# Computing k transposed, with its row sums on VectorE and a DMA transpose back to rows

## The chip, the cores and the metric

The kernel runs on one core of a Trainium2 chip. The metric is the device time of one execution in microseconds (us), of the slowest core (here there is only one). The profile's span is about 2 us shorter than that time.

## The reference, cut to what matters

A transformer block with adaptive layer norm: linear attention, then a gated feed-forward. Sequence 2048, width 1024, 32 heads of 32, bf16. The change concerns the attention's k:

```python
phi = lambda t: jnp.where(t > 0, t + 1, jnp.exp(t)) + 1e-06
pq, pk = (phi(q), phi(k))
kv  = jnp.einsum('bhsd,bhse->bhde', pk, v)
z   = jnp.einsum('bhsd->bhd', pk)                 # sum of phi(k) over all tokens
num = jnp.einsum('bhqd,bhde->bhqe', pq, kv)
den = jnp.einsum('bhqd,bhd->bhq', pq, z)[..., None] + 1e-06
o   = num / den
```

## The kernel before

A helper records every operation of every engine in program order, works out the semaphore waits from the tiles that they touch, and then emits each engine's list. So every engine, and the one DMA queue that SP feeds, works strictly in the recorded order. All profile lines carry the helper's line number (L178); tiles tell them apart.

The q/k stage works in four chunks of 512 tokens. For each chunk it needs `HT` (called h below): the normalised input (`XRES`, 128 tokens by 1024), transposed by four DMA transposes of 256 KB, then scaled and shifted tile by tile (8 tiles, 128x512), by VectorE and ScalarE. `HT` has two buffers, so h of chunk n+1 is prepared while chunk n is multiplied. A group is 8 matmuls of 128x512; a chunk is 8 groups for k, then 8 for q. Each group's PSUM bank is evacuated by ScalarE twice (exp and relu) and VectorE joins the two, for two groups at a time:

```python
def phi_flush():
    for i, dst in phi_pend:       # E1 = min(exp, 1) + 1e-6
        P.dve("tensor_scalar", out=E1[:, i, :], in0=E1[:, i, :], scalar1=1.0, scalar2=1e-6,
              op0=ALU.min, op1=ALU.add)
    for i, dst in phi_pend:       # phi = relu + E1
        P.dve("tensor_tensor", out=dst, in0=RL[:, i, :], in1=E1[:, i, :], op=ALU.add)
    ...
def k_group(ch, j, h):            # k by rows: tokens on partitions
    ...
    for dt in range(NDT):
        P.pe("matmul", out=PS[:, bank, :], lhsT=HT[:, buf, dt, j * 128:(j + 1) * 128],
             rhs=WQK[:, dt, lo:lo + 512], start=(dt == 0), stop=(dt == NDT - 1))
    phi_evac(bank, PKH[h][:, st, :])

def z_mm(st):                     # z: one-column matmuls against ones, 8 for each 128 tokens
    for hg in range(NHG):
        P.pe("matmul", out=PS[:, 6, 32 + hg:33 + hg], lhsT=PKH[hg // 4][:, st, (hg % 4) * 128:(hg % 4 + 1) * 128],
             rhs=ONES[:, 0:1], start=mcol_first[0], stop=(st == NST - 1), skip_group_check=True)
...
def late_loads():                 # called once, during chunk 0: 6 MB
    for ch in range(2, NCH):
        P.dma("x%d" % ch, XRES[:, 4 * ch:4 * ch + 4, :], xv[:, 4 * ch:4 * ch + 4, :])
    P.dma("stg0", STG[:], wmv[:, :, 2048:3072])
    P.dma("wv", WV[:], wqkvv[:, :, 2048:3072])
```

Between the groups stand side jobs, by group number. Those of chunk 1 that matter here: normalise the tokens of chunk 2 and send them to the DMA transpose (`ln1_xn`, `th_dma`, after groups 6 and 7), and scale the 8 tiles of h (`th_mod`, after groups 10 to 14). In chunk 2 the same for chunk 3, from group 1 on.

After the q/k stage come the products of k with the input (`pk`, called the attention products here), the denominator, the output projection and the feed-forward.

## Time and profile before

| | before |
|---|---|
| time, median | 840.5 us |
| TensorE busy | 829.9 of 837.9 us |
| VectorE busy | 299.7 us |
| one-column matmuls for z | 128, in 16 groups of 8 |

The engine table of the page (busy time, share of the span, instructions):

```profile
PE 829.9 (99%) x4241; PEld 383.6 (46%) x4241; DVE 299.7 (36%) x641; ACT 203.8 (24%) x355; POOL 40.9 (5%) x52
```

TensorE is the bound: 99% busy, and the chain of waits was 96% TensorE. The stage windows (columns: stretch, length, then busy time of PE, PEld, DVE, ACT and POOL with their instruction counts, granted clock, DMA share, GB/s) show that VectorE (DVE) is nevertheless close to full in parts of the q/k stage. The one before chunk 3:

```profile
89.70:103.90 14.20, 14.20 (x82) 6.64 (x81) 13.85 (x28) 11.12 (x20) 0.00 (x0) 1.00 0.12 31
```

The timeline of TensorE before (start, length, what; runs of like instructions merged, names are output, moving and stationary operand): the start of the last full-width q products of chunk 0, the start of chunk 2, one group for z, and the first attention product. The stretch between the first and the last of these lines, 26.26 to 132.94 = 106.68 us, is the yardstick. (Some expected texts below measure from the k products on, which start 28 matmuls later: 100.53 us before.)

```profile
26.26 6.31 PE L178 MATMUL ps<-ht,wqk 128*128 128x512 bf16 x28
...
75.45 8.80 PE L178 MATMUL ps<-wqk,ht 128*128 128x512 bf16 x40
...
91.39 0.24 PE L178 MATMUL ps<-ones,pk_87 128*128 128x1 bf16 x4
91.50 0.24 PE L178 MATMUL ps<-ones,pk_88 128*128 128x1 bf16 x4
91.60 3.61 PE L178 MATMUL ps<-ht,wqk 128*128 128x512 bf16 x16
...
132.94 2.32 PE L178 MATMUL ps<-pk_87,xres 128*128 128x512 bf16 x10
```

A group for z delays what follows from 91.39 to 91.60. The lengths printed for the matmuls are modelled and overlap; starts are what to count with.

How h of chunk 2 came in. The queue of SP first (the same kind of answer for the DMA issues; the length is that of the issuing), then VectorE's first scaling of that h:

```profile
59.97 2.61 SPq L178 DMA_TRANSPOSE ht<-xres  x2
```
```profile
63.58 3.66 SPq L178 DMA_TRANSPOSE ht<-xres  x2
```
```profile
69.17 0.41 DVE L178 TENSOR_SCALAR ht<-ht,modcol 128x512 bf16<-128x512 bf16 x1 [1.75 <-DMA ht<-xres]
```

The brackets say how long the engine was idle before that instruction, and for what. There was a gap in the queue between the two pairs of transposes, and VectorE waited 1.75 us for the last one to land. No TensorE wait followed from it: chunk 2 starts at 75.45 with 40 matmuls without a break.

### The profile page before, as it was taken

What the parts mean: (1) busy time and instruction counts of PE and PEld (TensorE: products, weight loads), DVE (VectorE), ACT (ScalarE), POOL (GpSimd) and SP (SyncE); (2) the same over time, 40 slices, a digit from 0 to 9 for tenths busy, and PEclk for the clock granted to TensorE, in tenths of its full rate; (3) what the DMA queues carried; (4) which work ended last, traced back from release to release, by engine and by line L of the source; (5) the groups of instructions that cost most, each with busy time, mean ns of one, the idle gap of its engine ahead of it and who ended that gap; (6) DMA issues with size and microseconds to landing.
All of it is one profiled execution on the core that took longest, in us unless ns stands there. A gap on an engine that the chain in (4) does not pass through costs nothing.

```text
span 837.9 us, 10302 instructions
## 1 busy us (share of the span) xinstructions
PE 829.9 (99%) x4241; PEld 383.6 (46%) x4241; DVE 299.7 (36%) x641; ACT 203.8 (24%) x355; POOL 40.9 (5%) x52
## 2 busy tenths in 40 slices
PE   7999999999999999999999999999999999999998
PEld 4444444454444444444444444444444444444444
DVE  5777966566984222111221112022121202111111
ACT  4667753223333111110111111021111111111111
POOL 1000000000050000030000003000000300000000
PEclk9999999999999999999999999999999999999999
DMA  9992323757096895530355562045557104553000
GB/s 283 265 322 48 75 77 127 162 147 273 29 251 187 254 308 154 154 73 26 111 153 151 151 162 58 20 114 151 151 151 181 45 13 114 151 152 98 1 25 26
DMA packets 178125, 112.99 MB, mean 135 GB/s; under 512 B 32664, under 2 KB 161824, under 8 KB 178080
## 3 DMA queue, kind: packets, MB, share of 16 engines
q1 hardware_dynamic: 178080, 112.35, 48.3%
q8 instruction: 33, 0.54, 0.3%
q14 instruction: 12, 0.10, 0.0%
HBM read 100.67 MB, written 4.33 MB: 125 GB/s over the span
## 4 chain that ended last, share of the span: by engine, by line
PE 96%; SPq 2%; DMA 1%; DVE 1%; issue 0%; ACT 0%; DVEq 0%
PE ps L178 96%; SPq L178 2%; DMA wsa<-in_w_mod_dram 1%; DVE acc L178 0%; DVE xres L178 0%; DVE mhl L178 0%; ACT mw L178 0%; DVE ve_72 L178 0%; DVE ut L178 0%; DVE mean_70 L178 0%; DVE msq_71 L178 0%; DVE sumx L178 0%; DVEq L249 0%
## 5 line engine op out<-in xcount | busy, mean ns | idle before, releaser
L178 DVE TENSOR_TENSOR at<-sg,ps 128x512 bf16<-128x512 bf16 x112 | 77.0, 687 | 296.2 <-PE ps L178 296.2
L178 ACT ACTIVATE sg<-ps 128x512 bf16<-128x512 f32 x112 | 66.9, 597 | 310.3 <-PE ps L178 310.3
L178 PE MATMUL ps<-wd_a,at 128*128 128x512 bf16 (+2 forms) x528 | 113.5, 373 | 0.0
L178 PE MATMUL ps<-wd_b,at 128*128 128x512 bf16 (+2 forms) x396 | 85.8, 373 | 0.0
L178 PEld LDWEIGHTS ps<-wd_a,at 128*128 128x128 bf16 x528 | 51.1, 98 | 59.8
L178 DVE TENSOR_TENSOR ut<-att,gb_b 128x512 bf16<-128x512 bf16 (+1 forms) x32 | 14.4, 451 | 166.7 <-ACT att L178 166.7
L178 ACT ACTIVATE att<-ps 128x512 bf16<-128x512 f32 (+1 forms) x32 | 17.4, 591 | 182.1 <-PE ps L178 182.1
L178 PE MATMUL ps<-ht,wqk 128*128 128x512 bf16 (+1 forms) x266 | 58.2, 371 | 0.6 <-DVE ht L178 0.6
L178 PEld LDWEIGHTS ps<-wd_b,at 128*128 128x128 bf16 x396 | 38.3, 98 | 44.7
L178 PE MATMUL ps<-wqk,ht 128*128 128x512 bf16 x256 | 57.4, 379 | 0.0
L178 PE MATMUL ps<-mw,pqt 128*128 128x512 bf16 x256 | 56.2, 379 | 0.1
L178 PE MATMUL ps<-h2t,gug_114 128*128 128x512 bf16 x224 | 52.9, 379 | 0.0
L178 PE MATMUL ps<-h2t,gug_111 128*128 128x512 bf16 x224 | 52.9, 379 | 0.0
L178 PE MATMUL ps<-h2t,guu_117 128*128 128x512 bf16 x224 | 52.9, 379 | 0.0
L178 PE MATMUL ps<-h2t,guu_116 128*128 128x512 bf16 x224 | 52.9, 379 | 0.0
L178 PE MATMUL ps<-h2t,guu_118 128*128 128x512 bf16 x224 | 52.9, 379 | 0.0
L178 PE MATMUL ps<-h2t,guu_115 128*128 128x512 bf16 x224 | 52.9, 379 | 0.0
L178 PE MATMUL ps<-h2t,gug_112 128*128 128x512 bf16 x224 | 52.9, 379 | 0.0
L178 PE MATMUL ps<-h2t,gug_113 128*128 128x512 bf16 x224 | 52.9, 379 | 0.0
L178 POOL TENSOR_SCALAR h2t<-h2t,modcol 128x512 bf16<-128x512 bf16 x32 | 28.2, 896 | 394.3 <-DMA h2t<-xn_119 394.3
L178 ACT ACTIVATE e_92<-ps 128x512 bf16<-128x512 f32 x64 | 39.1, 610 | 30.8 <-PE ps L178 26.9
L178 ACT ACTIVATE rl<-ps 128x512 bf16<-128x512 f32 x64 | 38.9, 608 | 0.0
(120 smaller groups left out, 686.9 us busy)
## 6 DMA issues: line engine op xcount, KB each, us to landing
gug_111<-in_B_w_gate_dram SPq DMA_DIRECT2D x14, 512.0 KB, 4.1
guu_115<-in_B_w_up_dram SPq DMA_DIRECT2D x14, 512.0 KB, 5.3
gug_112<-in_B_w_gate_dram SPq DMA_DIRECT2D x14, 512.0 KB, 4.0
guu_116<-in_B_w_up_dram SPq DMA_DIRECT2D x14, 512.0 KB, 5.3
gug_113<-in_B_w_gate_dram SPq DMA_DIRECT2D x14, 512.0 KB, 4.3
guu_117<-in_B_w_up_dram SPq DMA_DIRECT2D x14, 512.0 KB, 5.5
gug_114<-in_B_w_gate_dram SPq DMA_DIRECT2D x14, 512.0 KB, 4.1
guu_118<-in_B_w_up_dram SPq DMA_DIRECT2D x14, 512.0 KB, 5.3
```

The source lines that it names most:

```text
L178: return getattr(e, method)(**kw)
```

## The change

The intent: take the 16 groups of z matmuls off the bounding engine. If k is computed transposed, as q is, then the sum over tokens runs along the free dimension, and VectorE can produce it as a by-product of the last addition. But the attention products need k by rows, so each half chunk (4 groups, 512 KB) goes back through one DMA transpose. The loads of 6 MB are cut into pieces and spread, so that the transposes can pass between them.

```diff
+        PKT = [T("pkt%d" % i, o_, [128, 4, 4, 128], BF16) for i, o_ in enumerate((200 * KB, SM + 3072))]
+        ZP = T("zp", SM + 7808, [128, NHG, 4], FP32)
...
             for i, dst in phi_pend:
-                P.dve("tensor_tensor", out=dst, in0=RL[:, i, :], in1=E1[:, i, :], op=ALU.add)
+                if isinstance(dst, tuple):
+                    ch, nt = dst
+                    pkt = PKT[nt // 4]
+                    rows = lambda t_: t_[:, i, :].rearrange("p (j q) -> p j q", j=4)
+                    P.dve("scalar_tensor_tensor", out=pkt[:, :, nt % 4, :], in0=rows(RL), scalar=1.0, in1=rows(E1),
+                          op0=ALU.mult, op1=ALU.add, accum_out=ZP[:, nt, ch:ch + 1])
+                    if nt % 4 == 3:
+                        xbar(PKH[nt // 4][:, 4 * ch:4 * ch + 4, :].rearrange("p j (n d) -> p (j n) d", d=128),
+                             pkt[:].rearrange("p j n q -> p (j n q)"))
+                else:
+                    P.dve("tensor_tensor", out=dst, in0=RL[:, i, :], in1=E1[:, i, :], op=ALU.add)
...
-        def k_group(ch, j, h):
+        def k_group(ch, nt):
...
-                P.pe("matmul", out=PS[:, bank, :], lhsT=HT[:, buf, dt, j * 128:(j + 1) * 128],
-                     rhs=WQK[:, dt, lo:lo + 512], start=(dt == 0), stop=(dt == NDT - 1))
-            phi_evac(bank, PKH[h][:, st, :])
+                P.pe("matmul", out=PS[:, bank, :], lhsT=WQK[:, dt, D + nt * 128:D + (nt + 1) * 128],
+                     rhs=HT[:, buf, dt, :], start=(dt == 0), stop=(dt == NDT - 1))
+            phi_evac(bank, (ch, nt))
...  (z_mm and its calls go; z_cols reduces ZP over the chunks, late in chunk 3)
-        add(kside, 1, late_loads)
+        for i in range(4):
+            add(kside, i, lambda i=i: x_load(8 + i))          # 256 KB each
...
+        for i in range(4):
+            add(s1, 2 * i, lambda i=i: x_load(12 + i))
+        for i in range(NDT):
+            add(s1, 8 + i, lambda i=i: stg_load(i))
+            add(s2, 1 + i, lambda i=i: wv_load(i))
...  (two small modulation steps move to later places)
```

`s1`, `s2`, `s3` are the side jobs of chunks 1 to 3. The k transpose is recorded right after the last addition of its half chunk, so its place in the SP queue is fixed there. For chunk 1 that is between the second and the third of the h transposes for chunk 2.

More of the change, by code (lines that the diff above doesn't have):

```diff
@@ L330, in bass_adaLN_cond__linear_attn_block__swiglu_ffn__prompt_kernel @@
         MASK4 = T("mask4", SM + 2368, [128, 4], BF16)
-        BQ = T("bq", SM + 7808, [128, NDT], FP32)
         SUMXH = T("sumxh", SM + 2816, [128, NST, 2], FP32)
@@ L417, in bass_adaLN_cond__linear_attn_block__swiglu_ffn__prompt_kernel, with x_load, stg_load, wv_load @@
         P.dma("wk1", WQK[:, :, 1536:2048], wqkvv[:, :, 1536:2048])
-        def late_loads():
-            for ch in range(2, NCH):
-                P.dma("x%d" % ch, XRES[:, 4 * ch:4 * ch + 4, :], xv[:, 4 * ch:4 * ch + 4, :])
-            P.dma("stg0", STG[:], wmv[:, :, 2048:3072])
-            P.dma("wv", WV[:], wqkvv[:, :, 2048:3072])
+        def x_load(st):
+            P.dma("x%d" % st, XRES[:, st, :], xv[:, st, :])
+        def stg_load(kt):
+            P.dma("stg0_%d" % kt, STG[:, kt, :], wmv[:, kt, 2048:3072])
+        def wv_load(kt):
+            P.dma("wv%d" % kt, WV[:, kt, :], wqkvv[:, kt, 2048:3072])
         P.pool("memset", ap=IDENT[:], constant=1.0)
@@ L682, in q_group @@
             phi_evac(bank, PQT[:, nt, ch * 512:(ch + 1) * 512])
-        def k_group(ch, j, h):
-            st = 4 * ch + j
+        def k_group(ch, nt):
             buf, bank = ch % 2, next_bank()
-            lo = D + h * 512
             for dt in range(NDT):
-                P.pe("matmul", out=PS[:, bank, :], lhsT=HT[:, buf, dt, j * 128:(j + 1) * 128],
-                     rhs=WQK[:, dt, lo:lo + 512], start=(dt == 0), stop=(dt == NDT - 1))
-            phi_evac(bank, PKH[h][:, st, :])
-        mcol_first = [True]
+                P.pe("matmul", out=PS[:, bank, :], lhsT=WQK[:, dt, D + nt * 128:D + (nt + 1) * 128],
+                     rhs=HT[:, buf, dt, :], start=(dt == 0), stop=(dt == NDT - 1))
+            phi_evac(bank, (ch, nt))
         def macc(src, kt):
@@ L711, in mod_cols @@
                          rhs=ONES[:, 0:1], start=(m == 0 and i == 0), stop=(i == 1), skip_group_check=True)
-        def z_mm(st):
-            for hg in range(NHG):
-                P.pe("matmul", out=PS[:, 6, 32 + hg:33 + hg], lhsT=PKH[hg // 4][:, st, (hg % 4) * 128:(hg % 4 + 1) * 128],
-                     rhs=ONES[:, 0:1], start=mcol_first[0], stop=(st == NST - 1), skip_group_check=True)
-                mcol_first[0] = False
         def mod_fin_col(bank, c0, idx, plus_one):
@@ L807, in bass_adaLN_cond__linear_attn_block__swiglu_ffn__prompt_kernel @@
         q_phase_chunk0(qside)
-        gi = 0
-        for h in range(2):
-            for j in range(4):
-                k_group(0, j, h)
-                for f in kside.get(gi, []):
-                    f()
-                gi += 1
+        for gi in range(8):
+            k_group(0, gi)
+            for f in kside.get(gi, []):
+                f()
         def chunk(ch, side):
@@ L818, in chunk @@
                 if gi < 8:
-                    k_group(ch, gi // 2, gi % 2)
+                    k_group(ch, gi)
                 else:
@@ L823, in chunk, with z_cols @@
                     f()
-        s1, s2, s3 = {}, {}, {}
-        for j in range(4):
-            add(s1, 1 + j, lambda j=j: z_mm(j))
-            for ch, s_ in ((1, s1), (2, s2), (3, s3)):
-                add(s_, 4 + 2 * j, lambda st=4 * ch + j: z_mm(st))
+        def z_cols():
+            P.dve("tensor_reduce", out=ZCOL[:], in_=ZP[:], axis=mybir.AxisListType.X, op=ALU.add)
+            P.dve("tensor_copy", out=ZHL[:, 0, :], in_=ZCOL[:])
+            P.dve("tensor_tensor", out=ZHL[:, 1, :], in0=ZCOL[:], in1=ZHL[:, 0, :], op=ALU.subtract)
+            P.dve("tensor_tensor", out=ZSEL[:].rearrange("p (g x) -> p g x", x=36)[:, :, 0:4],
+                  in0=ZHL[:, 0, :].unsqueeze(2).to_broadcast([128, NHG, 4]),
+                  in1=MASK4[:].unsqueeze(1).to_broadcast([128, NHG, 4]), op=ALU.mult)
+        s1, s2, s3 = {}, {}, {}
+        for i in range(4):
[3 more added lines that the diff above has]
+            add(s2, 1 + i, lambda i=i: wv_load(i))
         ops = []
@@ L860, in bass_adaLN_cond__linear_attn_block__swiglu_ffn__prompt_kernel @@
         add(s3, 3, lambda: mod_row_a(7, 0, 0))
-        add(s3, 6, lambda: mod_row_b(7, 0, GA_B))
+        add(s3, 12, lambda: mod_row_b(7, 0, GA_B))
+        add(s3, 10, z_cols)
         chunk(1, s1)
@@ L865, in bass_adaLN_cond__linear_attn_block__swiglu_ffn__prompt_kernel @@
         phi_flush()
-        P.dve("tensor_copy", out=ZCOL[:], in_=PS[:, 6, 32:40])
         P.dma("wo", WO[:], wov)
-        P.dve("tensor_copy", out=ZHL[:, 0, :], in_=ZCOL[:])
-        P.dve("tensor_tensor", out=ZHL[:, 1, :], in0=ZCOL[:], in1=ZHL[:, 0, :], op=ALU.subtract)
-        P.dve("tensor_tensor", out=ZSEL[:].rearrange("p (g x) -> p g x", x=36)[:, :, 0:4],
-              in0=ZHL[:, 0, :].unsqueeze(2).to_broadcast([128, NHG, 4]),
-              in1=MASK4[:].unsqueeze(1).to_broadcast([128, NHG, 4]), op=ALU.mult)
         G_BANKS = [0] + [next_bank() for _ in range(4)]
@@ L977, in bass_adaLN_cond__linear_attn_block__swiglu_ffn__prompt_kernel @@
                 z_row()
+            if g == 1:
+                den()
+            if g == 3:
                 mod_cols(7, 0)
                 mod_fin_col(7, 0, 2, True)
-            if g == 1:
-                den()
             if 6 <= g <= 9:
```

## The prediction

> **What bounds it now.** TensorE. The engine table gives PE 829.9 us of an 837.9 us span (99%), at full granted clock; the chain of waits is 96% PE. VectorE (299.7 us, 36%) is off the chain on average, but windows of the q/k stage show it close: busy 17.4 of 18.8 us (28.4-47.2), 13.9 of 14.2 (89.7-103.9), 13.0 of 14.2 (118.7-132.9).
>
> **Removed.** The 128 one-column matmuls that sum k for z, 16 groups of 8. Their modelled 164 ns is not their cost: in the timeline a group pushes the next matmul back by 0.20 to 0.21 us (91.39 to 91.60), so PE loses 16 x 0.207 = 3.3 us. That is all TensorE gains: k transposed has as many 128x512 matmuls, at the same 0.216 us spacing.
>
> **Added.** (a) VectorE: 32 tensor_tensor adds (128x512 bf16, 0.335 us start to start) become scalar_tensor_tensor with an accumulator. The existing one of that size (residual, from PSUM) takes 687 ns plus an 83 ns accumulator read, 0.645 us start to start: about one element per cycle. The Trainium skill ("VectorE: DVE Perf Modes", "The perf-mode tier table") gives bf16 tensor_tensor 2x and does not list this operation. So +0.31 us each, 2.5 us per chunk, 10 us in all. (b) 8 DMA transposes of 512 KB. The 256 KB ones issue in 1.3 us and land after 3.2; the 1 MB ones 5.3-7.4 and 7-8. So about 2.7 us of issue, 4.5-5 to landing. They share the one in-order SP queue with the h transposes; the bulk loads are cut small so that they pass between.
>
> **On the critical path.** The 3.3 us count in full. Against them stand deadlines for VectorE at chunk starts:
> - Chunk 1: the last h scaling ends at 46.95 us; PE wants it at 46.2 + 1.5 = 47.7. Six slower adds lie ahead of it, less 0.8 us that VectorE idled for the h transpose: ends about 47.9. PE stall 0.2-0.4 us.
> - Chunk 2: scaling waits for the last h transpose (69.17 us). A k transpose now stands between the second and third of the four in the queue (+2.7 us); SP had idled there, so some is hidden: landing about 70-71. Then 5.7 us of VectorE up to its last tile, about 76; PE wants that at about 75.4. Stall 0.3-1.2 us.
> - Chunk 3: VectorE finishes about 1 us early. No stall.
> - The k rows are read at 130 and 160 us; transposes land about 10 us before. z and denominator are no later. No stall.
>
> Everything after 133 us is unchanged and merely starts earlier.
>
> **Prediction.** 840.5 - 3.3 + 1.0 = 838.2 us, range 836.8 to 840.4. Chances: faster by over 2% 0.01, within 2% 0.97, slower 0.02.
>
> **What would show it.** One-column matmuls with k gone, PE busy down about 3.3 us; k adds at 650-770 ns, VectorE busy up about 10 us; new transposes landing in 4-6 us; PE idle of a few tenths at 46-48 us and up to 1 us at 74-76 us, released by VectorE or ScalarE writing h; the first attention product starting 2-3 us earlier (132.9 before); the feed-forward stage unchanged in length.
>
> **What would make it wrong.** The 3.3 us surviving whole (queues deeper than I counted: 837); k transposes much slower than scaled from the h ones, delaying h at chunks 2 and 3 by several us (841-844); the accumulating add not being one element per cycle; a transpose into k landing after 130 us.

## The result, and the profile after

| | before | after |
|---|---|---|
| time, median (range) | 840.5 us (839.92 to 840.84) | 839.63 us (839.31 to 840.76) |
| yardstick stretch | 106.68 us | 105.78 us |
| TensorE busy | 829.9 us | 827.7 us |
| VectorE busy | 299.7 us | 306.1 us |

The ratio is 0.9993, 95% interval 0.9975 to 1.001: no difference that four runs show. The same kernel run again in five rounds gave 839.70 us against 840.65, ratio 0.9992 (0.998 to 1.0005). The feed-forward is unchanged: from the first attention product to the first feed-forward product it takes 121.40 us in both profiles (132.94 to 254.34, and 132.61 to 254.01).

The engine table after:

```profile
PE 827.7 (99%) x4113; PEld 380.2 (45%) x4113; DVE 306.1 (37%) x673; ACT 203.0 (24%) x355; POOL 41.1 (5%) x52
```

TensorE in the yardstick stretch after (132.61 - 26.83 = 105.78 us):

```profile
26.83 49.34 PE L178 MATMUL ps<-ht,wqk 128*128 128x512 bf16 x226
77.37 27.80 PE L178 MATMUL ps<-ht,wqk 128*128 128x512 bf16 x128 [1.20 <-DVE ht L178]
105.61 4.06 PE L178 MATMUL ps<-ht,wqk 128*128 128x512 bf16 x18 [0.44 <-DVE ht L178]
...
132.61 3.62 PE L178 MATMUL ps<-pk_89,xres 128*128 128x512 bf16 x16
```

The z matmuls are gone, but the stream now breaks twice, both times for a scaled h tile: in the first k group of chunk 2 (77.37) and of chunk 3 (105.61). How much each costs follows from the starts. In the runs without a break (a1 to a4 below) the seventh matmul of chunk 2 starts 48.88 us after the start of the stretch and that of chunk 3 after 76.52 (76.51 to 76.53). Here the first came after 50.54 us: 1.66 us late. The second came after 78.78: 2.26 us late, so 0.60 more. (The brackets show less. The printed lengths of matmuls overlap by about 0.16 us, and at chunk 2 the sixth matmul, whose tile ScalarE scales, was already 0.28 us late.)

Why h was late. The queue of SP after, during chunks 1 and 2:

```profile
60.82 2.70 SPq L178 DMA_TRANSPOSE ht<-xres  x2
63.57 3.34 SPq L178 DMA_TRANSPOSE pk_90<-pkt_75  x1
66.95 2.69 SPq L178 DMA_TRANSPOSE ht<-xres  x2
...
84.32 1.24 SPq L178 DMA_TRANSPOSE ht<-xres  x1
85.60 2.73 SPq L178 DMA_TRANSPOSE pk_89<-pkt_74  x1
88.38 0.58 SPq L178 DMA_DIRECT2D wv<-in_A_wqkv_dram  x1
89.00 1.24 SPq L178 DMA_TRANSPOSE ht<-xres  x1
90.28 0.58 SPq L178 DMA_DIRECT2D wv<-in_A_wqkv_dram  x1
90.91 1.24 SPq L178 DMA_TRANSPOSE ht<-xres  x1
```

The gap in the middle of the h transposes has been filled by a k transpose (`pk_90<-pkt_75`), and the five are issued back to back from 60.82 to 69.64. The last h transpose itself lands 3.2 us after its issue, against 3.1 before, so what delays it is the wait for its turn. VectorE waits for their end:

```profile
71.59 0.41 DVE L178 TENSOR_SCALAR ht<-ht,modcol 128x512 bf16<-128x512 bf16 x1 [4.73 <-DMA ht<-xres]
...
76.91 0.41 DVE L178 TENSOR_SCALAR ht<-ht,modcol 128x512 bf16<-128x512 bf16 x1
```
```profile
94.57 0.41 DVE L178 TENSOR_SCALAR ht<-ht,modcol 128x512 bf16<-128x512 bf16 x1 [1.50 <-DMA ht<-xres]
```

At 71.59 it has idled 4.73 us, against 1.75 before. It then needs until 77.32 to come to the last h tile that it scales, and TensorE takes that up at 77.37. In chunk 2 it idles another 1.50 us, where before it had not waited at all.

### The profile page after: what moved, and what is told of

Read it like the earlier page. It is cut to its first block, busy times and chain, and to the rows that moved or that the text cites. A ratio compares the mean times of both kernels' runs of the same rounds, so it can differ in the third digit from the quotient of the medians.

```text
span 837.6 us, 10117 instructions
## 1 busy us (share of the span) xinstructions
PE 827.7 (99%) x4113; PEld 380.2 (45%) x4113; DVE 306.1 (37%) x673; ACT 203.0 (24%) x355; POOL 41.1 (5%) x52
## 4 chain that ended last, share of the span: by engine, by line
PE 91%; DVE 4%; SPq 2%; DMA 2%; issue 1%; ACT 0%; DVEq 0%; ACTq 0%
PE ps L178 91%; SPq L178 2%; DVE acc L178 1%; DMA wsa<-in_w_mod_dram 1%; DMA ht<-xres 1%; DVE xres L178 0%; DVE stats L178 0%; DVE pqt L178 0%; DVE ht L178 0%; DVE e_94 L178 0%; DVE mhl L178 0%; DVE pkt_75 L178 0%; ACT e_94 L178 0%; ACT mw L178 0%; DVE mv L178 0%
## 5 line engine op out<-in xcount | busy, mean ns | idle before, releaser
L178 PE MATMUL ps<-ht,wqk 128*128 128x512 bf16 (+1 forms) x522 | 112.8, 375 | 2.4 <-DVE ht L178 2.2
L178 PEld LDWEIGHTS ps<-ht,wqk 128*128 128x128 bf16 x522 | 50.2, 98 | 62.8 <-DVE ht L178 4.0
```

Of the source, the lines that this page charges most:

```text
L178: return getattr(e, method)(**kw)
```

## The experiments

Theory Q, when they were planned: the k transposes stand in front of the h transposes in the in-order queue, so h lands late. Theory V: the accumulating adds, which start every 0.61 us where the plain ones start every 0.335, make VectorE late. "Wrong on purpose" means that z or k has false values. The comparison with the reference passed even these runs, so it does not see the attention branch here; a pass says little about k in any of the runs below.

Positions in the following table are in us after the start of the yardstick stretch. "h issued" is the first h transpose for chunk 2, "h scaled" the start and the end of VectorE's scaling of it. TensorE wants the last of these tiles at 48.88 (the eighth tile is ScalarE's). All positions are of one profiled execution for each run. "Stalls" are computed from the starts as above. Each job's runs have their own times before on the same chip: 840.60 us for a1 to a4, 840.65 for the repeated changed kernel, b1, a5 and a7, 840.78 for a6 and a8; the first is shown.

| run | time, us | ratio | stretch | h issued | h scaled | stall chunk 2 | chunk 3 |
|---|---|---|---|---|---|---|---|
| before | 840.6 | 1 | 106.68 | | | | |
| after | 839.63 | 0.9993 | 105.78 | 33.99 | 44.76-50.49 | 1.66 | 0.60 |
| after again | 839.70 | 0.9992 | 106.13 | 34.41 | 45.08-50.81 | 1.37 | 0.64 |
| a1 h first | 837.54 | 0.9961 | 103.49 | 33.98 | 42.01-47.74 | 0 | 0 |
| a2 plain adds | 837.31 | 0.9959 | 103.53 | 32.67 | 42.81-48.54 | 0 | 0 |
| a3 no k transposes | 837.30 | 0.9959 | 103.50 | 34.07 | 41.53-47.25 | 0 | 0 |
| a4 neither | 837.43 | 0.9957 | 103.50 | 32.71 | 40.72-46.45 | 0 | 0 |
| b1 before without z | 837.40 | 0.9964 | 104.06 | | | | |
| a5 h first in chunk 1 | 838.09 | 0.9971 | 103.94 | 34.04 | 41.99-47.72 | 0 | 0.42 |
| a6 plain adds in chunk 1 | 838.32 | 0.9974 | 104.49 | 32.66 | 43.41-49.13 | 0.3 | 0.7 |
| a8 v loads later | 838.93 | 0.9979 | 104.65 | 33.81 | 44.25-49.96 | 1.14 | 0 |
| a7 loads in bulk | 853.26 | 1.0151 | | | | | |

### a1: the h transposes first

```diff
                     if nt % 4 == 3:
-                        xbar(PKH[nt // 4][...], pkt[...])
+                        def go(ch=ch, h=nt // 4, pkt=pkt):
+                            xbar(PKH[h][...], pkt[...])
+                        if (ch, nt // 4) in ((1, 1), (2, 0)):
+                            k_pend.append(go)       # sent by k_send
+                        else:
+                            go()
...
+        add(s1, 7, k_send)       # after the last h transpose for chunk 2
+        add(s2, 4, k_send)       # after the last h transpose for chunk 3
```

> The changed kernel, with two of the eight k transposes (second half of chunk 1, first half of chunk 2) put behind the h transposes of the same stretch in the SP queue. Nothing else moves. Theory Q (the new transposes stand in front of the h transposes in the one in-order queue, so h lands late): VectorE's wait for h at about 71.6 us goes from 4.7 us back to about 2 us, that at 94.6 us from 1.5 us to nothing, PE's stall at the start of chunk 2 falls from 1.7 us to 0.5 or less and that of chunk 3 from 0.6 us to 0.2 or less; the time falls by 1.5 to 2 us against the changed kernel. Theory V (the slower accumulating adds make VectorE late): both stalls stay and the time is that of the changed kernel within 0.4 us.

```profile
26.96 80.56 PE L178 MATMUL ps<-ht,wqk 128*128 128x512 bf16 x372
...
130.45 3.62 PE L178 MATMUL ps<-pk,xres 128*128 128x512 bf16 x16
```
```profile
60.94 5.73 SPq L178 DMA_TRANSPOSE ht<-xres  x4
66.71 2.07 SPq L178 DMA_TRANSPOSE pk<-pkt  x1
```
```profile
68.97 0.41 DVE L178 TENSOR_SCALAR ht<-ht,modcol 128x512 bf16<-128x512 bf16 x1 [1.98 <-DMA ht<-xres]
```

The three answers are TensorE's timeline, SP's and VectorE's. TensorE now runs 372 full-width matmuls without a break. (Buffer numbers are missing from the names in this trace.) The stretch is 103.49 us. VectorE waits 1.98 us for h and not at all in chunk 3, as theory Q had it; theory V is refuted as a theory of the adds alone. This version only reorders two transposes of the changed kernel, with the waits worked out by the same helper; it beats both kernels: 0.9961 of the time before (0.9948 to 0.9973), against 0.9992 (0.998 to 1.0005) for the changed kernel in five rounds on another chip.

### a2, a3, a4: one suspect at a time, and neither

a2 puts a plain add in place of the accumulating one, with the same layout:

```diff
-                    P.dve("scalar_tensor_tensor", out=pkt[:, :, nt % 4, :], in0=rows(RL), scalar=1.0, in1=rows(E1),
-                          op0=ALU.mult, op1=ALU.add, accum_out=ZP[:, nt, ch:ch + 1])
+                    P.dve("tensor_tensor", out=pkt[:, :, nt % 4, :], in0=rows(RL), in1=rows(E1), op=ALU.add)
```

(and fills ZP with a constant). a3 lets the add write straight to the k tile and drops the transposes:

```diff
-                    pkt = PKT[nt // 4]
+                    pkt = PKH[nt // 4][:, 4 * ch:4 * ch + 4, :].rearrange("p j (n d) -> p j n d", d=128)
...
-                    if nt % 4 == 3:
-                        xbar(...)
```

a4 does both.

> The changed kernel with the 32 accumulating adds turned back into plain adds of the same shape and layout; z is then a constant, so the result is wrong on purpose. The k transposes stay. Theory Q: the stalls at the starts of chunks 2 and 3 remain for the most part (1.3 us or more at chunk 2), the time falls by less than 0.7 us. Theory V: VectorE is 10 us less busy and both stalls go, the time falls by about 2 us.

> The changed kernel without the eight k transposes: the accumulating adds write straight into the tile that the transposes fill, so its content is not transposed and the result is wrong on purpose. Theory Q: as the run that puts h first, stalls at chunks 2 and 3 together 0.7 us or less, time lower than the changed kernel by 1.5 to 2 us. Theory V: unchanged within 0.4 us.

> Both at once: plain adds and no k transposes (wrong on purpose). Both theories expect no stall left: PE gets the whole 3.3 us, from the start of the k products of chunk 0 to the first attention product it takes 97.2 us (before 100.5 us), and the time is about 837.3 us. If stalls remain here, both theories miss a cause, for instance the bulk loads that were cut into pieces.

TensorE's timeline for a2, which was the surprise:

```profile
26.44 80.59 PE L178 MATMUL ps<-ht,wqk 128*128 128x512 bf16 x372
...
129.97 3.62 PE L178 MATMUL ps<-pk,xres 128*128 128x512 bf16 x16
```

VectorE and SP in a2, around h of chunk 2:

```profile
69.25 0.41 DVE L178 TENSOR_SCALAR ht<-ht,modcol 128x512 bf16<-128x512 bf16 x1 [3.04 <-DMA ht<-xres]
...
91.94 0.41 DVE L178 TENSOR_SCALAR ht<-ht,modcol 128x512 bf16<-128x512 bf16 x1 [2.03 <-DMA ht<-xres]
```
```profile
59.11 2.60 SPq L178 DMA_TRANSPOSE ht<-xres  x2
62.10 2.19 SPq L178 DMA_TRANSPOSE pk<-pkt  x1
64.33 2.98 SPq L178 DMA_TRANSPOSE ht<-xres  x2
```

The last tile that VectorE scales for chunk 2, in a3 and in a4:

```profile
73.41 0.41 DVE L178 TENSOR_SCALAR ht<-ht,modcol 128x512 bf16<-128x512 bf16 x1
```
```profile
73.16 0.41 DVE L178 TENSOR_SCALAR ht<-ht,modcol 128x512 bf16<-128x512 bf16 x1
```

All three have no stall left (103.50 to 103.53 us). So theory Q missed a2, and theory V missed a1 and a3: neither suspect alone costs anything; together they cost 2.3 us. The table shows how. In a4 the last h tile that VectorE scales is ready at 46.45, which is 2.4 us before TensorE wants it. That is the slack of this chunk start. Slow adds alone (a3 against a4) use up 0.80 us of it, k transposes alone (a2 against a4) 2.09 us, both together 4.04 us, which is 1.6 more than there is. The stall measured was 1.66 us. Read this way the finish of the scaling gives the stall at chunk 2 within 0.1 us in every run for which the table has it. (In the second execution of the changed kernel a load had held TensorE for 0.58 us near the start, so that it wanted the tile at 49.46.)

The margins are small, though. At the start of chunk 3 in a2 VectorE finished at 76.47, and TensorE wanted that tile at 76.53: the k transposes alone came within 0.06 us of costing something there.

The sum of the two, 2.89 us, is already more than the slack; together they took 1.15 us more still. The queue shows two parts of this extra. Without the k transpose, the queue idles between the two pairs of h transposes; a late first pair then costs nothing further, and of the 1.36 us by which slow adds delay the first issue (34.07 against 32.71) only 0.81 reach the scaling. With it, the five issues are back to back, and the whole 1.32 us (33.99 against 32.67) goes through; a6 below shows the same with the adds of chunk 1 alone, 1.33 us at the issue and 1.36 at the end of the scaling. The other part is in the queue after the first issue: 10.77 us to the scaling in the changed kernel, 10.14 in a2, which had a gap of 0.4 us ahead of the k transpose and issued it in 2.19 instead of 3.34 us. The adds of chunk 1 do not explain this part: a6, with the same first issue as a2, took 10.75 us and 3.08 us for that issue. It also varies by itself: the changed kernel again and a8, which do not differ from it up to this point, took 10.67 and 10.44. What sets it no run here shows.

### b1: the kernel before, without z

```diff
-            for hg in range(NHG):
+            for hg in (range(NHG) if st == 0 else ()):
...                               (the one group left gets stop=True)
```

> The kernel before, with 15 of its 16 groups of one-column z matmuls left out (z is then wrong on purpose) and nothing else changed. If the whole gain of the change is these matmuls, the stretch from the first full-width k product to the first attention product shortens by 15 x 0.207 = 3.1 us, and the time falls to 837.2 to 837.6, as the runs without stall gave. If k transposed had a gain of its own (another spacing of the matmuls), this run would fall short of those.

837.40 us, ratio 0.9964: as good as any run without stall. The profiled execution had one wait of 0.18 us for a load of q/k weights in the stretch, which cost 0.34 us by the starts; 104.06 less that and less the one z group left in is 103.5, the stretch of a1. So the whole gain is the z matmuls, and k transposed has none of its own. It measures 106.68 - 103.50 = 3.18 us, 24.8 ns for each one-column matmul. The Trainium skill ("VectorE: DVE Perf Modes", the errata section) gives a matmul as the larger of 60 and 6 + columns cycles at 2.4 GHz; for one column that makes 25 ns, an estimate.

### a5, a6, a8: whether the two chunk starts are separate, and where the lateness enters

a5 is a1 with only the transpose of chunk 1 moved. a6 has plain adds in chunk 1 only (and a constant in ZP at the start). a8 moves the eight v loads:

```diff
-                        if (ch, nt // 4) in ((1, 1), (2, 0)):        # a5, against a1
+                        if (ch, nt // 4) == (1, 1):

+                    if ch == 1:                                      # a6, against the changed kernel
+                        P.dve("tensor_tensor", ...)                  # the plain add of a2
+                    else:
                         P.dve("scalar_tensor_tensor", ...)

-            add(s2, 1 + i, lambda i=i: wv_load(i))                   # a8, against the changed kernel
+            add(s2, 8 + i, lambda i=i: wv_load(i))
```

> The changed kernel unaltered, to have it on the same chip and in the same rounds: 839.6 within 0.4 us, stalls of 1.7 us at chunk 2 and 0.6 us at chunk 3 again.

> The changed kernel with only one of the two k transposes put behind the h transposes, that of chunk 1. The theory after the first four runs: queue and slow adds each use up part of one slack of about 2.4 us at each chunk start, and only their sum exceeds it; the two chunk starts are separate. Then the stall at chunk 2 goes (0 to 0.2 us) and the one at chunk 3 stays at 0.5 us or more, since PE arrives there as early as VectorE: time 838.0 to 838.7. Rival: the stall at chunk 3 is only a consequence of the one at chunk 2; then both go and the time is 837.5.

> The changed kernel with plain adds in chunk 1 only (8 of 32; part of z is then a constant, wrong on purpose); the k transposes are all in their old places. If the slow adds matter by making the head of the back-to-back queue late (first h transpose issued 34.0 us after the start of the long product stretch, against 32.7 with plain adds throughout), then 8 plain adds in chunk 1 bring that first issue forward by 0.6 us or more, and the stall at chunk 2 falls from 1.7 us to 0.7 us or less, while that at chunk 3 stays at 0.4 us or more: time 838.0 to 838.8. If the adds matter only later, in the scaling itself, the stall at chunk 2 stays above 1.2 us.

> The changed kernel with the eight 256 KB loads of the v weights moved behind the h transposes of chunk 2 (each takes 0.58 us of issue between them). The k transposes stay where they were. The queue theory expects h of chunk 3 about 1 us earlier, the stall at chunk 3 down from 0.6 to 0.2 us or less, the one at chunk 2 unchanged at 1.7 us: time 839.0 to 839.4. The rival, that only the k transposes matter in the queue, expects no change (839.7).

The changed kernel again: 839.70 us, stalls of about 1.4 (1.7 was expected) and 0.6 us. So the size of the first varies by some tenths between executions; here a load near the start of the stretch had held TensorE for 0.58 us, so that it came to chunk 2 later. TensorE's timeline of a5:

```profile
26.66 76.67 PE L178 MATMUL ps<-ht,wqk 128*128 128x512 bf16 x347
103.60 4.06 PE L178 MATMUL ps<-ht,wqk 128*128 128x512 bf16 x17 [0.27 <-DVE ht L178]
...
130.60 3.62 PE L178 MATMUL ps<-pk,xres 128*128 128x512 bf16 x16
```

The stall at chunk 2 is gone, that at chunk 3 stays, 0.42 us (expected 0.5 or more). So it is not a consequence of the first: each chunk start has a slack of its own. In a6 the first h transpose is issued 1.3 us earlier and the stall at chunk 2 falls to 0.3 us with the k transpose still in its place: the slow adds matter by making the head of the queue late. The k transpose of a6 in the queue of SP, and then TensorE in a8 from the end of its stall at chunk 2 on:

```profile
62.40 3.08 SPq L178 DMA_TRANSPOSE pk<-pkt  x1
```
```profile
78.33 31.69 PE L178 MATMUL ps<-ht,wqk 128*128 128x512 bf16 x146 [0.98 <-DVE ht L178]
```

In a8 the 146 matmuls run through the start of chunk 3 without a break, although the k transpose stayed where it was: the small v loads between the h transposes (0.58 us of issue each) were part of that queue, not only the k transposes. Its time, 838.93 us, is a little below the expected 839.0 to 839.4. Why is not shown: its stall at chunk 2 was only 1.14 us, but in the slowest of its five executions (840.11 us), which is the one profiled.

### a7: the loads in bulk again

```diff
-        for i in range(4):
-            add(kside, i, lambda i=i: x_load(8 + i))
+        add(kside, 1, late_loads)
...                               (the other small loads go as well)
```

> The changed kernel with the loads of x, of the modulation weights and of the v weights issued early and whole, as in the kernel before (6 MB at once at about 41 us), instead of in 256 KB pieces. If the pieces are needed, the first k transposes wait behind 6 MB (12 to 17 us at the 350 to 410 GB/s that single loads reached), chunk 1 cannot write its k tile, VectorE idles 5 us or more on it and PE stalls at chunk 1: time over 841 us. If they are not needed: 839.6 within 0.5 us.

VectorE waiting for the k tile; then, from the stage windows, TensorE's granted clock (the third column from the right, 0.75 and 0.50) during a second, longer break (79.52 to 84.53) and later:

```profile
64.63 0.69 DVE L178 SCALAR_TENSOR_TENSOR pkt<-rl,e 128x512 bf16<-128x512 bf16 x1 [11.94 <-DMA pk<-pkt]
```
```profile
79.30:84.50 5.20, 0.22 (x2) 0.00 (x0) 1.04 (x4) 0.46 (x1) 0.00 (x0) 0.75 0.81 154
```
```profile
89.80:95.60 5.80, 5.76 (x14) 2.10 (x15) 3.33 (x11) 3.23 (x7) 1.01 (x1) 0.50 0.01 3
```

853.26 us, 1.5% slower than before; over 841 was expected if the pieces are needed. The first k transpose waits behind 6 MB and lands after 16.8 us instead of 4.2 to 5.4; VectorE has to wait before it overwrites the source of that transpose, and idles 11.94 us; everything behind it is late, h too, and TensorE has breaks, the longest of 2.7 and 5.0 us. After the second its granted clock is 0.50 for over 10 us, so that the matmuls of that time start every 0.427 us, half as often. The Trainium skill ("TensorE: Matmul & The Clock Gate", "What's actually happening") says that the clock is gated to half after at least one idle window of about 3.4 us. This trace agrees in part: the 2.7 us break was followed by no such drop, the 5.0 us one by 0.50. But the mean of 0.75 over the window above puts the drop in the middle of the break, about 2.4 us after the last matmul (the same view gives 1.00 from 79.5 to 81.9 us and 0.51 from 81.9 to 84.5). So here less than 3.4 us without a matmul was enough.

So the change would lose time with the loads in bulk; cutting them is a necessary part of it.

## Why the prediction was right or wrong

The time was in the range: 838.2 predicted, 839.63 measured. That alone says little. The range reached from a gain of 0.1 us to one of 3.7, and a step of this size could hardly leave the 2%; the gain was forecast as 2.3 us and measured as 0.9, which is within the noise of four runs. The outline of the mechanism was right, a gain on TensorE with part of it given back as waits for h at chunk starts. Where the waits fall and how large they are was not. Point by point:

- The 3.3 us removed: 3.18 us, shown by b1 and by the four runs without stall.
- "+0.31 us each" for the accumulating adds: they start 0.61 us apart, against 0.335 before, so 0.28 each, and take 682 ns plus 80. 32 x 0.28 is 8.8 us; VectorE busy rose by 6.4 us and not by 10, because other groups covered less time (the min of E1 15.9 us instead of 17.3, for instance: one takes 281 ns instead of 286, and more of them overlap).
- 512 KB transposes: issue 1.7 to 3.6 us, landing in 4.2 to 5.4, where about 2.7 and 4.5 to 5 were said. Right. (The 1 MB transposes it scaled from land after 7.0 to 9.4 us in the trace, not 7 to 8.)
- Chunk 1, "PE stall 0.2-0.4 us": none. The scaling ended at 48.1, TensorE wanted it at 48.3 in that trace.
- Chunk 2, "Stall 0.3-1.2 us": 1.66 us. The landing was as estimated (71.5, or 70.9 on the time scale of before, where 70-71 was said); the scaling then ended 0.75 us later than "about 76", on that scale, and TensorE wanted the tile at 75.15, not at 75.4.
- Chunk 3, "VectorE finishes about 1 us early. No stall": this step failed. It names VectorE's work alone, and not that a k transpose and the v loads stand between the h transposes for chunk 3 too. VectorE waited 1.50 us for h and TensorE stalled 0.60. a1 and a8 show it: with the k transpose behind the h transposes, or with the v loads moved, the stall is gone. The queue alone was not enough here either: in a2 VectorE waited 2.03 us and TensorE not at all.
- "transposes land about 10 us before" the k rows are read: the last two land at 118.3 and 125.9 us, the rows are read from 132.6 and 162.9 on, and no TensorE wait for them appears in any trace.

So of the terms of the sum, the 1.0 us given back was mis-sized: it measured 2.3 us. What the prediction did not see is that its two costs share one slack. Taken one at a time, each of them cost nothing, at chunk 3 by a hair.

## What to carry to other kernels

When work leaves the bounding engine, list the deadlines that its feeders must meet and the slack at each, and add up all that the change puts ahead of one deadline: two costs can each be free and together not. In an in-order DMA queue put what is needed soon ahead of what is needed late, even if it becomes ready later: moving two transposes, whose data were read tens of microseconds later, gave 2 us back. Here a queue with gaps absorbed part of the lateness at its head (0.81 of 1.36 us went through), and one nearly without gaps passed all of it on (1.33 us at the issue, 1.36 at the end of the scaling).

## What the Trainium skill lacked or had wrong

- "VectorE: DVE Perf Modes", the perf-mode tier table, does not list scalar_tensor_tensor. Here 128x512 bf16 from SBUF with an accumulator took 682 ns plus 80 ns for the accumulator read and started every 0.61 us; the bf16 tensor_tensor of the same size took 418 ns and started every 0.335 us, in a2 with the same output layout too. The sum is thus not free. Whether the operation or its accumulator makes the difference no run separates.
- "DMA: Bandwidth & Descriptors" gives a bandwidth for DMA transposes, and sequencer cycles for two other shapes in its part on trn3, but not how long one of these sizes holds the issuing queue: mostly 1.2 to 1.4 us for 256 KB (up to 2.3 in the changed kernel), 1.7 to 3.6 us for 512 KB, and 14.6 us behind 6 MB of loads (a7).
- The same page, rules for kernel authors, says that a transpose next to ordinary DMAs "needs nothing". That is about correctness, which no run here tests for k. It lacks the cost in time: a transpose behind 6 MB of loads landed after 16.8 us instead of 4.2 to 5.4.
